# Softcap attention followed by a gated mixture of attention experts: q, k and x transposed by DMA instead of by TensorE and VectorE

## The chip, the cores and the metric

The kernel runs on one NeuronCore of a Trainium2 chip. A core has TensorE (PE, matrix products; PEld are its weight loads), VectorE (DVE), ScalarE (ACT), GpSimd (POOL) and SyncE (SP), which here only issues DMAs. Every engine works through its own instructions in order, and engines wait for each other by semaphores. DMAs are issued from an engine's instruction queue (here from SyncE and, for the weights, from GpSimd) and run on 16 DMA engines. The metric is the device time of one execution in microseconds. The time before is 442.53 us, the median of three runs (442.25 to 444.14).

## What is computed

There are 8 batches, 12 heads, 448 tokens and 64 values per head. The first part is attention with a soft cap: `scores = cap * tanh(q k^T / (8 * cap))`, with cap 30, a softmax over the keys, and a product with `v`. Its output, with the heads laid side by side, is `x`, 448 x 768 per batch. The second part works on `x`:

```python
logits = x @ w_gate                  # 4 experts, the best two kept, softmax over the two
for e in range(E):
    q, k, v = x @ wq[e], x @ wk[e], x @ wv[e]      # 64 wide
    a = softmax(causal(q @ k.T / 8))
    out += weight[e] * (a @ v @ wo[e])
```

Inputs and output are float32; the kernel computes its matrix products in float16.

## The kernel before

Work of the first part goes by pairs of heads: six pairs per batch, 48 pairs, numbered p. A main loop runs over p, one iteration per pair and a few more at the end, and the order of instructions on each engine is the order in which the program writes them (a manual schedule). Work of the second part, here called the MoE part, of batch b is cut into units (`b_v`, `b_gate`, `b_q`, `b_k`, score fills, `b_pv1`, `b_ot`, `b_wo`). A table in `batch_b` spreads these over the iterations that follow the last pair of that batch, so they run among the pairs of the next batch. Each iteration has two places for units: `w1`, between the two score fills of a pair, and `w2`, after the normalisation. After the last pair the units of the last batch run alone; this is the tail.

For one pair the steps are these.

- `load` brings q, k and v of one batch to SBUF by seven DMAs on SyncE's queue (batch 0 in four groups of seven). Four tokens of q, and three of k, lie beside each other on a partition, so that a partition reads one contiguous run. The last 64 keys of both heads come separately (`ktf`). Two sets of buffers alternate. The load of batch b + 1 is written at the start of the first iteration of batch b.
- `a_cast(p)` on GpSimd turns one pair's q, k and v to float16. It is written in iteration p - 3.
- `a_tr(p)`, written in iteration p - 2, transposes q (four products on TensorE), the tail keys (one) and k (three) into a PSUM tile `tps`. VectorE copies that to `qt` and, once per head, to a zeroed tile `kz`: the two heads share the 128 rows, so a head's keys must stand beside zeros.
- `fill0` and `fill1` compute the scores of the two heads on TensorE, four and three products with 448 columns, into the one score buffer in PSUM (four banks). `tanh` and `expo` on ScalarE turn them into unnormalised probabilities: 128 x 1792 values for the first head with both heads' tail keys, 128 x 1344 for the second.
- `a_pv` multiplies by v, with a column of ones for the sums, and `a_norm` on VectorE divides.
- `a_xt` transposes the normalised pair `xk` by four products on TensorE into `xtp`, and VectorE copies it to `xT` (line 281), with the tokens put back into their natural order: the copy writes every fourth column.

The MoE units read `xT` as soon as the last pair of a batch is there. The small PSUM tiles (`tps`, `xtp`, and all of the MoE part except its scores) take turns in two buffers. The MoE scores use the same score buffer as `fill0` and `fill1`. `b_wo` writes the output: VectorE copies to `ob`, and SyncE's queue stores it.

Of the kernel before, what the change touches and what calls it, by code (L numbers as in the profile page):

```python
# [8 lines left out]
f32 = mybir.dt.float32  # L9
f16 = mybir.dt.float16  # L10
# [6 lines left out]
def kernel(  # L17
# [13 lines left out]
    nc = tc.nc  # L31

    B, H, S, Dh = q.shape
# [62 lines left out]
    ident = const.tile([128, 128], f16, name="ident")  # L96
# [12 lines left out]
    for i in range(2):  # L109
        nc.gpsimd.memset(ktz[i], 0.0)  # L110
    for i in range(3):
        nc.vector.memset(kz[i], 0.0)
# [13 lines left out]
    cast = {}  # L126

    def a_cast(p):
        if p >= NP:
            return  # L130
        b, j = divmod(p, HP)
        qf, kf, vf, ktf, vtf = staged[b]
        h0 = 2 * j
        q16 = hd.tile([QP, QC, 2, Dh], f16, name=f"q16_{p}", tag="q16")
        k16 = hd.tile([128, KC, 2, Dh], f16, name=f"k16_{p}", tag="k16")
# [17 lines left out]
        cast[p] = (q16, k16)  # L153

    qkt = {}

    def a_tr(p):
        if p >= NP:
            return
        b, j = divmod(p, HP)  # L160
        q16, k16 = cast.pop(p)
        tps = ps_aux.tile([128, 1024], f16, name=f"tps_{p}", tag="aux")
        for c in range(QC):
            nc.tensor.transpose(  # L164
                tps[:, c * QP : (c + 1) * QP],
                q16[:, c, :, :].rearrange("p h d -> p (h d)"),
                ident[0:QP, 0:QP],
            )
        nc.tensor.transpose(tps[:, S : S + 128], ktz[b % 2][:, j, :], ident)
        for c in range(KC):  # L170
            nc.tensor.transpose(  # L171
                tps[:, S + 128 * (c + 1) : S + 128 * (c + 2)],
                k16[:, c, :, :].rearrange("p h d -> p (h d)"),
                ident,
            )
        qt = hd.tile([128, S + 128], f16, name=f"qt_{p}", tag="qt")
        nc.vector.tensor_copy(qt, tps[:, 0 : S + 128])  # L177
# [3 lines left out]
        qkt[p] = (qt, kk)  # L181

    score = {}

    def fill0(p):
        if p >= NP:
            return
        qt, kk = qkt[p]
        sc = ps_score.tile([128, 4, 512], f32, name=f"s0_{p}", tag="score")
        for c in range(KC):  # L190
            nc.tensor.matmul(  # L191
                sc[:, c, 0:S], kk[:, 0, 128 * c : 128 * (c + 1)], qt[:, 0:S],
                start=True, stop=True,
            )
        nc.tensor.matmul(sc[:, 3, 0:S], qt[:, S : S + 128], qt[:, 0:S], start=True, stop=True)  # L195
        score[(p, 0)] = sc

    def fill1(p):
        qt, kk = qkt.pop(p)
        sc = ps_score.tile([128, 4, 512], f32, name=f"s1_{p}", tag="score")  # L200
        for c in range(KC):
            nc.tensor.matmul(  # L202
                sc[:, c, 0:S], kk[:, 1, 128 * c : 128 * (c + 1)], qt[:, 0:S],
                start=True, stop=True,
            )
        score[(p, 1)] = sc

    y = {}
    pr = {}
# [53 lines left out]
        xt[p] = xk  # L263

    xT = {}

    def transpose4(ps, src):

        for n in range(4):
            nc.tensor.transpose(  # L270
                ps[:, 128 * n : 128 * (n + 1)], src(n), ident if n < 3 else swap
            )

    def a_xt(p):
        b, j = divmod(p, HP)
        if j == 0:
            xT[b] = xp.tile([128, NDC, S], f16, name=f"xT_{b}", tag="xT")
        xk = xt.pop(p)
        ps = ps_aux.tile([128, 512], f16, name=f"xtp_{p}", tag="aux")
        transpose4(ps, lambda n: xk[:, n, :, :].rearrange("p g d -> p (g d)"))  # L280
        nc.vector.tensor_copy(  # L281
            xT[b][:, j, :].rearrange("m (p c) -> m c p", c=QC),
            ps[:, 0:S].rearrange("m (c p) -> m c p", c=QC),
        )


# [160 lines left out]


    a_cast(0)
    a_cast(1)  # L450

# [30 lines left out]
    def batch_b(b):  # L482

        f = lambda fn, *a: (lambda: fn(*a))
        tab = {
            0: ([f(b_v, b, 0)], [f(b_v, b, 1), f(b_v, b, 2)]),
            1: ([f(b_v, b, 3)], [f(b_gate, b), f(b_q, b, 0)]),
            2: ([f(b_k, b, 0)], [("S", b, 0)]),
            3: ([f(b_q, b, 1)], [f(b_k, b, 1)]),
            4: ([f(b_pv1, b, 0), f(b_pv1, b, 1)], [("S", b, 1)]),  # L490
            5: (
                [f(b_pv1, b, 2), f(b_pv1, b, 3)],
                [f(b_ot, b, 0), f(b_ot, b, 1), f(b_wo, b, 0)],
            ),
            6: ([f(b_wo, b, 1)], []),
            7: ([f(b_wo, b, 2)], [f(b_wo, b, 3)]),
        }
        return tab

    sched = {}  # L500
    for b in range(B):
        for s_, (w1, w2) in batch_b(b).items():
            e_ = sched.setdefault(HP * (b + 1) + 1 + s_, ([], []))
            e_[0].extend(w1)
            e_[1].extend(w2)

    def run(units):
        for u in units:
            u()

    a_tr(0)
    a_cast(2)
    weights(0)
    a_tr(1)
    fill0(0)
    last = max(sched)
    for p in range(last + 1):
        w1, w2 = sched.get(p, ([], []))
        sB = [u for u in w2 if isinstance(u, tuple)]
        w2 = [u for u in w2 if not isinstance(u, tuple)]  # L520
        b, j = divmod(p, HP)
        if j == 0 and b + 1 < B:
            load(b + 1, [(0, HP)])
        if p < NP:
            tanh(p, 0)
            fill1(p)
        if 1 <= p <= NP:
            expo(p - 1, 1)
            a_pv(p - 1, 0)
        a_tr(p + 2)  # L530
        a_cast(p + 3)
        if 1 <= p < 4:
            weights(p)
        run(w1)
        if p < NP:
            tanh(p, 1)
        if not sB:
            fill0(p + 1)
            if p < NP:
                expo(p, 0)  # L540
        else:
            for _, bb, r in sB:
                b_fill(bb, r)
            if p < NP:
                expo(p, 0, 0, 2)
            for _, bb, r in sB:
                b_exp(bb, r)
            fill0(p + 1)
# [43 lines left out]
```

## Time and profile before

| | before |
|---|---|
| median of three runs | 442.53 us |
| the profiled execution | 441.75 us, its span 440.0 us |
| granted TensorE clock, mean | 0.939 |
| first big tanh (pair 0) starts at | 11.66 us |
| the tail, from about | 395 us |
| DMA queue of SyncE | 52,944 packets, 44.05 MB, 34.3% of 16 engines |
| VectorE, copies of `qt`, `kz` (two) and `xT` | 22.3, 16.2, 17.3 and 55.9 us |
| GpSimd idle before its q casts | 205.1 us |

The span runs from the first instruction to the last. A row of the profile's groups gives a line and an engine, what is written from what, shape and count, then the busy time, the mean of one in nanoseconds, and the idle time of that engine before these instructions with what ended it. Idle time of an engine that isn't the bottleneck costs nothing.

### The profile page before, as it was taken

How to read it: one execution, taken by the hardware profiler on the slowest of the kernel's cores; microseconds unless marked ns; L12 is line 12 of the kernel's file. 1: busy time of each engine (PE TensorE's matmuls, PEld its weight loads, DVE VectorE, ACT ScalarE, POOL GpSimd, SP SyncE). 2: the span in 40 equal slices, each digit the busy share in tenths (PEclk: the TensorE clock that was granted, in tenths of full speed). 3: DMA queues.
4: the chain of work that ended last, by engine and by line, in shares of the span. 5: the costliest groups of instructions: out<-in, count | busy, mean ns of one | idle time of the engine just before them, and what ended most of it. 6: DMA issues, size and time to landing. Idle time of an engine off the chain costs nothing.

```text
span 440.0 us, 8813 instructions
## 1 busy us (share of the span) xinstructions
PE 311.9 (71%) x3568; PEld 205.7 (47%) x3568; DVE 276.6 (63%) x693; ACT 305.7 (69%) x231; POOL 132.8 (30%) x374
## 2 busy tenths in 40 slices
PE   2676686857759677667868587686776678686865
PEld 1354464545535454444536454355544455354442
DVE  6145476567836588468755678365884687557745
ACT  1779797987757777788758877578767887584030
POOL 6793973233223323223322332233232220000000
PEclk9999899899977999999997999779999999979896
DMA  5999998001191012900184012910110001000303
GB/s 139 282 238 229 247 266 253 2 2 72 59 324 51 1 73 80 336 17 37 74 251 144 1 73 65 332 35 2 72 55 3 1 36 72 19 1 9 118 1 125
DMA packets 63497, 46.19 MB, mean 105 GB/s; under 512 B 24288, under 2 KB 59872, under 8 KB 63456
## 3 DMA queue, kind: packets, MB, share of 16 engines
q1 hardware_dynamic: 52944, 44.05, 34.3%
q0 software_dynamic: 10512, 1.58, 4.8%
q8 instruction: 28, 0.46, 0.5%
q14 instruction: 13, 0.11, 0.1%
HBM read 36.19 MB, written 11.01 MB: 107 GB/s over the span
## 4 chain that ended last, share of the span: by engine, by line
PE 45%; DVE 29%; ACT 10%; SPq 6%; issue 5%; DMA 3%; POOL 1%; DVEq 0%; ACTq 0%; POOLq 0%
PE pv L245 8%; PE s L191 6%; ACT pB L389 6%; DVE ob L443 5%; PE kps L357 4%; PE s L202 4%; DVE xT L281 4%; DVE xk L257 4%; PE vps L300 3%; PE sB L378 3%; PE qps L347 3%; PE xtp L270 2%; PE wops L438 2%; DVE kzB L361 2%; DVE kz L180 2%
## 5 line engine op out<-in xcount | busy, mean ns | idle before, releaser
L215 ACT ACTIVATE y<-s 128x1792 f16<-128x1792 f32 x96 | 141.8, 1477 | 53.6 <-PE s L195 33.5
L226 ACT ACTIVATE p<-y 128x1792 f16<-128x1792 f16 (+2 forms) x110 | 147.2, 1339 | 0.0
L136 POOL CAST q<-qf 112x512 f16<-112x512 f32 x48 | 29.5, 614 | 205.1 <-PE tps L164 176.8
L245 PEld LDWEIGHTS <-p 128*128 128x128 f16 x1536 | 66.6, 103 | 21.8 <-issue 6.2
L245 PE MATMUL pv<-v,p 128*128 128x65 f16 x1152 | 66.2, 201 | 0.8 <-ACT p L226 0.8
L281 DVE COPY xT<-xtp 128x448 f16<-128x448 f16 x48 | 55.9, 1164 | 11.4 <-PE xtp L270 11.1
L389 ACT ACTIVATE pB<-sB 128x1984 f16<-128x1984 f32 x16 | 29.2, 1824 | 46.2 <-PE sB L383 46.2
L191 PE MATMUL s<-qt,kz 128*128 128x448 f16 x144 | 40.7, 397 | 27.1 <-ACT pB L389 24.9
L245 PE MATMUL pv<-vtz,p 128*128 128x65 f16 x384 | 58.8, 199 | 0.0
L255 DVE RECIPROCAL rc<-pv 128x8 f32<-128x8 f32 x48 | 10.0, 208 | 75.6 <-PE pv L245 75.6
L438 PE MATMUL wops<-wo,oT 128*128 128x384 f16 x128 | 32.2, 348 | 18.2 <-DVE kz L180 10.3
L177 DVE COPY qt<-tps 128x576 f16<-128x576 f16 x48 | 22.3, 465 | 33.8 <-PE tps L171 33.7
L202 PE MATMUL s<-qt,kz 128*128 128x448 f16 x144 | 39.7, 389 | 4.9 <-ACT y L215 4.8
L443 DVE COPY ob<-wops 128x384 f32<-128x384 f32 (+1 forms) x64 | 34.6, 557 | 5.6 <-PE wops L438 4.6
L257 DVE TENSOR_TENSOR xk<-pv,rc 128x512 f16<-128x512 f32 x48 | 33.2, 692 | 1.7
L270 PE MATMUL xtp<-ident,xk 128*128 128x128 f16 x144 | 17.2, 232 | 23.4 <-DVE xk L257 20.6
L191 PEld LDWEIGHTS <-kz 128*128 128x128 f16 x144 | 14.7, 106 | 38.8 <-issue 32.9
L164 PE MATMUL tps<-ident,q 112*128 112x112 f16 x192 | 19.1, 227 | 13.2 <-POOL q L136 9.3
L270 PEld LDWEIGHTS <-xk 128*128 128x128 f16 x192 | 12.6, 102 | 33.9 <-DVE xk L257 25.9
L347 PE MATMUL qps<-xT,wq 128*128 128x448 f16 x96 | 23.3, 384 | 5.9 <-DVE ob L443 5.8
L300 PE MATMUL vps<-wvg,xT 128*128 128x260 f16 x192 | 26.5, 283 | 1.0
L146 POOL CAST v<-vf 128x384 f16<-128x384 f32 x48 | 24.4, 507 | 8.9 <-DMA vf<-in_v_dram 6.2
(86 smaller groups left out, 510.9 us busy)
## 6 DMA issues: line engine op xcount, KB each, us to landing
qf<-in_q_dram SPq DMA_DIRECT2D x7, 1344.0 KB, 8.5
out_dram<-ob SPq DMA_DIRECT2D x24, 384.0 KB, 2.3
kf<-in_k_dram SPq DMA_DIRECT2D x7, 1152.0 KB, 10.8
vf<-in_v_dram SPq DMA_DIRECT2D x7, 1152.0 KB, 8.3
out_dram<-ob SPq DMA_DIRECT2D x8, 192.0 KB, 2.7
ktf<-in_k_dram SPq DMA_DIRECT2D x14, 96.0 KB, 9.4
vtf<-in_v_dram SPq DMA_DIRECT2D x14, 96.0 KB, 6.8
qf<-in_q_dram SPq DMA_DIRECT2D x2, 448.0 KB, 5.1
```

The costliest lines, as they stand in the source:

```text
L191: nc.tensor.matmul(sc[:, c, 0:S], kk[:, 0, 128 * c : 128 * (c + 1)], qt[:, 0:S], start=True, stop=True,)
L202: nc.tensor.matmul(sc[:, c, 0:S], kk[:, 1, 128 * c : 128 * (c + 1)], qt[:, 0:S], start=True, stop=True,)
L215: nc.scalar.activation(yt, sc[:, 0:n, 0:S], AF.Tanh, scale=isc / capf)
L226: nc.scalar.activation(pt[:, c0:c1, :], yt[:, c0:c1, :], AF.Exp, scale=capf)
L245: nc.tensor.matmul(pv[:, g, 65 * n : 65 * n + 65], lhsT, rhs, start=(c == 0), stop=(c == KC),)
L257: nc.vector.tensor_tensor(xk.rearrange("p n g d -> p g n d"), pv[:, :, :, 0:64], rc.broadcast_to((128, 2, 4, Dh)), ALU.mult,)
L270: nc.tensor.transpose(ps[:, 128 * n : 128 * (n + 1)], src(n), ident if n < 3 else swap)
L281: nc.vector.tensor_copy(xT[b][:, j, :].rearrange("m (p c) -> m c p", c=QC), ps[:, 0:S].rearrange("m (c p) -> m c p", c=QC),)
L300: nc.tensor.matmul(ps, xT[b][:, j, WIN[n] : WIN[n] + 128], wvg[:, j, :], start=(j == 0), stop=(j == NDC - 1))
L389: nc.scalar.activation(pb[:, 64:2048], s.pop(("sc", r))[:, 0:1984], AF.Exp, scale=isc)
L438: nc.tensor.matmul(ps, s["oT"][r][:, w : w + 128], wo2[r][:, f * (D // 2) : (f + 1) * (D // 2)], start=(r == 0), stop=(r == 1),)
L443: nc.vector.tensor_copy(ob[lo:128, f * (D // 2) : (f + 1) * (D // 2)], ps[lo:128, :])
```

## The change

`a_tr` no longer uses TensorE, PSUM and VectorE. It issues two transposing DMAs on SyncE's queue: one for q (112 partitions x 512 columns), one for k (128 x 896). So that the transposed keys stand beside zeros, the zeros are put in before: a constant tile `kin` (three buffers, set to zero once by VectorE) has seven blocks of 128 columns, three per head and one for the tail keys of both, and `a_cast` on GpSimd writes the keys of a head into its half of the columns. The cast of k is thereby two instructions instead of one. `fill` reads `kt` (7 blocks) and `qt` where these DMAs land.

`a_xt` issues two transposing DMAs, one for the first three windows of tokens (128 x 384) and one for the last 64 tokens, to a new tile `xp`. A new step `a_xu`, on GpSimd and one iteration later, copies `xp` to `xT` and restores the order of the tokens. The MoE table is written anew: its units come half an iteration later, the last ones closer together, and within an iteration `a_xt` now stands before the units of `w2`. Ahead of the loop `a_tr(1)` moves before `a_cast(2)`.

```diff
-    ktz = [const.tile([128, HP, 128], f16, name=f"ktz{i}") for i in range(2)]
+    kin = [const.tile([128, 7, 128], f16, name=f"kin{i}") for i in range(3)]
-    kz = [const.tile([128, 2, KM], f16, name=f"kz{i}") for i in range(3)]
...
     def a_cast(p):
-        nc.gpsimd.tensor_copy(
-            k16, kf[:, h0 : h0 + 2, :].rearrange("p h (c d) -> p c h d", c=KC)
-        )
-        kt = ktz[b % 2]
-        nc.gpsimd.tensor_copy(kt[0:64, j, 0:Dh], ktf[0:64, j, :])
-        nc.gpsimd.tensor_copy(kt[64:128, j, Dh:128], ktf[64:128, j, :])
+        kk = kin[p % 3]
+        for g in range(2):
+            nc.gpsimd.tensor_copy(
+                kk[:, KC * g : KC * (g + 1), Dh * g : Dh * (g + 1)],
+                kf[:, h0 + g, :].rearrange("p (c d) -> p c d", c=KC),
+            )
+            nc.gpsimd.tensor_copy(
+                kk[64 * g : 64 * (g + 1), 2 * KC, Dh * g : Dh * (g + 1)],
+                ktf[64 * g : 64 * (g + 1), j, :],
+            )
...
     def a_tr(p):
-        tps = ps_aux.tile([128, 1024], f16, name=f"tps_{p}", tag="aux")
...
-        qt = hd.tile([128, S + 128], f16, name=f"qt_{p}", tag="qt")
-        nc.vector.tensor_copy(qt, tps[:, 0 : S + 128])
-        kk = kz[p % 3]
-        nc.vector.tensor_copy(kk[0:64, 0, :], tps[0:64, S + 128 : S + 512])
-        nc.vector.tensor_copy(kk[64:128, 1, :], tps[64:128, S + 128 : S + 512])
+        q16 = cast.pop(p)
+        qt = hd.tile([128, S], f16, name=f"qt_{p}", tag="qt")
+        nc.sync.dma_start_transpose(
+            qt.rearrange("m (c p) -> m c p", c=QC), q16.rearrange("p c h d -> p (c h d)")
+        )
+        kt = hd.tile([128, 7, 128], f16, name=f"kt_{p}", tag="kt")
+        nc.sync.dma_start_transpose(kt, kin[p % 3].rearrange("p c m -> p (c m)"))
...
     def a_xt(p):
-        ps = ps_aux.tile([128, 512], f16, name=f"xtp_{p}", tag="aux")
-        transpose4(ps, lambda n: xk[:, n, :, :].rearrange("p g d -> p (g d)"))
-        nc.vector.tensor_copy(
+        xp_ = hd.tile([128, S], f16, name=f"xp_{p}", tag="xp")
+        nc.sync.dma_start_transpose(
+            xp_[:, 0:KM].rearrange("m (n t) -> m n t", n=3),
+            xk[:, 0:3, :, :].rearrange("p n g d -> p (n g d)"),
+        )
+        nc.sync.dma_start_transpose(
+            xp_[:, KM:S].unsqueeze(1), xk[64:128, 3, :, :].rearrange("p g d -> p (g d)")
+        )
+        xun[p] = xp_
+
+    def a_xu(p):
+        b, j = divmod(p, HP)
+        nc.gpsimd.tensor_copy(
             xT[b][:, j, :].rearrange("m (p c) -> m c p", c=QC),
-            ps[:, 0:S].rearrange("m (c p) -> m c p", c=QC),
+            xun.pop(p).rearrange("m (c p) -> m c p", c=QC),
         )
...
         a_tr(p + 2)
         a_cast(p + 3)
+        if 2 <= p <= NP + 1:
+            a_xu(p - 2)
...
             a_pv(p - 1, 1)
             a_norm(p - 1)
-        run(w2)
         if 1 <= p <= NP:
             a_xt(p - 1)
+        run(w2)
```

More of the change, by code (lines that the diff above doesn't have):

```diff
@@ L108 @@
     pB = [const.tile([128, 64 + 1984], f16, name=f"pB{i}") for i in range(2)]
-    for i in range(2):
-        nc.gpsimd.memset(ktz[i], 0.0)
     for i in range(3):
-        nc.vector.memset(kz[i], 0.0)
+        nc.vector.memset(kin[i], 0.0)
     for i in range(2):
@@ L134, in a_cast @@
         q16 = hd.tile([QP, QC, 2, Dh], f16, name=f"q16_{p}", tag="q16")
-        k16 = hd.tile([128, KC, 2, Dh], f16, name=f"k16_{p}", tag="k16")
         nc.gpsimd.tensor_copy(
@@ L152, in a_cast @@
         nc.gpsimd.tensor_copy(vt_[64:128, j, 1, 0:Dh], vtf[64:128, j, :])
-        cast[p] = (q16, k16)
+        cast[p] = q16
     qkt = {}
@@ L159, in a_tr @@
             return
-        b, j = divmod(p, HP)
-        q16, k16 = cast.pop(p)
-        tps = ps_aux.tile([128, 1024], f16, name=f"tps_{p}", tag="aux")
[L163 to L175, printed above, removed]
@@ L176, in a_tr @@
-        qt = hd.tile([128, S + 128], f16, name=f"qt_{p}", tag="qt")
-        nc.vector.tensor_copy(qt, tps[:, 0 : S + 128])
-        kk = kz[p % 3]
-        nc.vector.tensor_copy(kk[0:64, 0, :], tps[0:64, S + 128 : S + 512])
-        nc.vector.tensor_copy(kk[64:128, 1, :], tps[64:128, S + 128 : S + 512])
-        qkt[p] = (qt, kk)
+        q16 = cast.pop(p)
[3 more added lines that the diff above has]
+        )
@@ L183, with fill @@
+        kt = hd.tile([128, 7, 128], f16, name=f"kt_{p}", tag="kt")
+        nc.sync.dma_start_transpose(kt, kin[p % 3].rearrange("p c m -> p (c m)"))
+        qkt[p] = (qt, kt)
     score = {}
-    def fill0(p):
+    def fill(p, g):
         if p >= NP:
             return
-        qt, kk = qkt[p]
-        sc = ps_score.tile([128, 4, 512], f32, name=f"s0_{p}", tag="score")
+        qt, kt = qkt[p]
+        sc = ps_score.tile([128, 4, 512], f32, name=f"s{g}_{p}", tag="score")
         for c in range(KC):
[L191 to L206, printed above, removed]
+            nc.tensor.matmul(sc[:, c, 0:S], kt[:, KC * g + c, :], qt, start=True, stop=True)
+        if g == 0:
+            nc.tensor.matmul(sc[:, KC, 0:S], kt[:, 2 * KC, :], qt, start=True, stop=True)
@@ L208 @@
+        score[(p, g)] = sc
     y = {}
@@ L265 @@
     xT = {}
+    xun = {}
     def transpose4(ps, src):
@@ L484, in batch_b @@
         f = lambda fn, *a: (lambda: fn(*a))
[L485 to L497, printed above, removed]
+        tab = [
+            [],
+            [f(b_v, b, 0), f(b_v, b, 1)],
+            [f(b_v, b, 2), f(b_v, b, 3)],
+            [f(b_gate, b), f(b_q, b, 0)],
+            [f(b_k, b, 0)],
+            [("S", b, 0)],
+            [f(b_q, b, 1)],
+            [f(b_k, b, 1)],
+            [f(b_pv1, b, 0), f(b_pv1, b, 1)],
+            [("S", b, 1)],
+            [f(b_pv1, b, 2), f(b_pv1, b, 3)],
+            [f(b_ot, b, 0), f(b_ot, b, 1), f(b_wo, b, 0), f(b_wo, b, 1)],
+            [f(b_wo, b, 2), f(b_wo, b, 3)],
+        ]
         return tab
@@ L501 @@
     for b in range(B):
[L502 to L505, printed above, removed]
+        for i, units in enumerate(batch_b(b)):
+            sched.setdefault(2 * (HP * (b + 1) + 1) + i, []).extend(units)
     def run(units):
@@ L511 @@
     a_tr(0)
+    a_tr(1)
     a_cast(2)
     weights(0)
-    a_tr(1)
-    fill0(0)
-    last = max(sched)
+    fill(0, 0)
+    last = max(sched) // 2
     for p in range(last + 1):
-        w1, w2 = sched.get(p, ([], []))
+        w1, w2 = sched.get(2 * p, []), sched.get(2 * p + 1, [])
         sB = [u for u in w2 if isinstance(u, tuple)]
@@ L525 @@
             tanh(p, 0)
-            fill1(p)
+            fill(p, 1)
         if 1 <= p <= NP:
@@ L537 @@
         if not sB:
-            fill0(p + 1)
+            fill(p + 1, 0)
             if p < NP:
@@ L547 @@
                 b_exp(bb, r)
-            fill0(p + 1)
+            fill(p + 1, 0)
             if p < NP:
```

## The prediction

> **What bounds the kernel now.** First the page's table of busy time by engine.
>
> ```profile
> PE 311.9 (71%) x3568; PEld 205.7 (47%) x3568; DVE 276.6 (63%) x693; ACT 305.7 (69%) x231; POOL 132.8 (30%) x374
> ```
>
> Three engines stand near 70% and none is full, so I read ScalarE's own timeline, away from the MoE work and inside it. Columns: start, length, engine, line, what, and idle time before it.
>
> ```profile
> 33.22 1.31 ACT L226 ACTIVATE p<-y 128x1344 f16<-128x1344 f16 x1
> 34.43 1.28 ACT L215 ACTIVATE y<-s 128x1344 f16<-128x1344 f32 x1
> 35.60 1.70 ACT L226 ACTIVATE p<-y 128x1792 f16<-128x1792 f16 x1
> 37.19 1.66 ACT L215 ACTIVATE y<-s 128x1792 f16<-128x1792 f32 x1
> 38.73 1.33 ACT L226 ACTIVATE p<-y 128x1344 f16<-128x1344 f16 x1
> ```
>
> Here one head pair takes 38.73 - 33.22 = 5.5 us and ScalarE never waits: PE and VectorE, transposes included, are wholly behind it. The big tanh of pairs 36 to 42, with MoE work between, starts at 301.40, 307.23, 315.57, 322.92, 335.46, 340.99 and 350.44: 49.0 us for six pairs. ScalarE's own work there is 6 x 5.5 plus two MoE exponentials at 1.8, 36.7 us. The other 12.3 us are waits, the same as in the list of waits (us in total, times, longest):
>
> ```profile
> ACT pB L389 <- PE sB L383: 46.2, 16, 5.7
> ACT y L215 <- PE s L195: 33.5, 34, 9.6
> ACT eexp L322 <- DVE lg L311: 21.1, 7, 12.3
> SPq L446 <- DVE ob L443: 280.5, 25, 33.9
> ```
>
> So only iterations with MoE work can be shortened, up to 12 us per batch. The last line matters as much: today the SyncE queue does nothing but load and store, waits 280 us for stores, and so runs its loads far ahead. The SyncE timeline:
>
> ```profile
> 17.62 0.59 SPq L74 DMA_DIRECT2D qf<-in_q_dram  x1
> ...
> 34.62 0.89 SPq L90 DMA_DIRECT2D vtf<-in_v_dram  x1
> ...
> 119.27 0.54 SPq L74 DMA_DIRECT2D qf<-in_q_dram  x1
> 119.90 0.71 SPq L77 DMA_DIRECT2D kf<-in_k_dram  x1
> 120.70 3.79 SPq L82 DMA_DIRECT2D ktf<-in_k_dram  x1
> 124.55 1.94 SPq L83 DMA_DIRECT2D ktf<-in_k_dram  x1
> 126.60 1.30 SPq L84 DMA_DIRECT2D vf<-in_v_dram  x1
> 128.41 2.31 SPq L89 DMA_DIRECT2D vtf<-in_v_dram  x1
> 130.78 0.61 SPq L90 DMA_DIRECT2D vtf<-in_v_dram  x1
> ```
>
> One batch's load holds SyncE 12.1 us (four such: 10.9 to 12.3, so 11.5), about 340 GB/s for its 4.1 MB. The load at 119.27 belongs to iteration 18, whose tanh starts at 147.80: it ran 28 us ahead, and cost nobody anything.
>
> **What the change removes.** VectorE loses, per pair, 0.465 (qt) + 0.338 + 0.361 (kz) + 1.164 (xT) = 2.33 us, 112 us of its 277. PE loses twelve transposes; by the pieces of the chain (tps 0.20 + 0.06 + 0.18, xtp 0.38) 0.82 us per pair. Rows:
>
> ```profile
> L281 DVE COPY xT<-xtp 128x448 f16<-128x448 f16 x48 | 55.9, 1164 | 11.4 <-PE xtp L270 11.1
> L177 DVE COPY qt<-tps 128x576 f16<-128x576 f16 x48 | 22.3, 465 | 33.8 <-PE tps L171 33.7
> ```
>
> What that is worth lies between 0 and 12.3 us per batch. What stays behind ScalarE is the chain in the iterations with an MoE score fill: kps 1.15, kzB 0.62 + 0.23 (+ 0.55), sB 1.4, of which the half exponential covers 0.95. I leave 2 us of waits for each of the two and a little for the rest: 4.3 us remain, 8 go, and a batch would take 41 us if the transposes cost nothing.
>
> **What it adds on GpSimd.** The k cast in two (from the 64- and 384-column casts, 0.23 and 0.51 us, 0.35 each at 192: +0.2) and the reordering copy, 448 columns: 0.6 us by the cast rows, 1.5 if the strided writes hurt as on VectorE (1.16 against 0.46 for more columns). 2.6 us per pair become 3.4 to 4.3, below 5.5; GpSimd idles 205 us before its q casts. Taken as hidden. Its new wait (x landed) has the next pair's casts behind it; they are needed over an iteration later. If that cover went, it would be 1 us per pair, 48 in all.
>
> **What it adds on SyncE.** Four transposing DMAs per pair, and no row shows one. A 128-column block of two-byte values is 256 B per row: q has 112 x 4 = 448 such pieces, k 128 x 7 = 896, x 128 x 3 + 64 = 448; 1,792 in all, 0.46 MB. Low end: by bytes at the load's 340 GB/s, 1.35 us per pair moving, with issue at 0.6 us each (startup rows: 0.39 to 0.66), 2.4 us of SyncE. High end: the 256 B pieces of the ktf load at its worst, 4.32 us for 384, 11.25 ns each, 20 us per pair; that row is mostly back-pressure of the loads ahead. Between them lies the nearest row of small packets:
>
> ```profile
> q0 software_dynamic: 10512, 1.58, 4.8%
> ```
>
> 4.8% of 16 x 440 us is 338 us, 32 ns per packet of 150 B, 2.0 ns over 16 engines: 3.6 us per pair. I take it, and that SyncE is held while a transpose's pieces are pushed: q 1.5, k 2.4, x 1.4 + 0.7, 6.0 us per pair; landing 2 us later (2.3 for a store).
>
> Against this stand two statements of the Trainium skill that disagree. Its page Advanced Engine Details and Errata, section X-Bar Transpose (TRN2), holds transposing DMAs as fast as others, 350 to 400 GB/s: an estimate of 1.3 us per pair, and a result near 436. Its page VectorE: DVE Perf Modes, section The three transpose paths, gives 1309 ns for one 128x128 block by DMA against 390 on TensorE, and tells authors to use TensorE where PSUM will do: 14 blocks per pair would be 18 us, an estimated 1,000 us in all. No row here shows either.
>
> **Where it meets the path.** SyncE works in order. The x transposes wait for VectorE's normalisation late in the iteration, and behind them stand the next load, the next pair's q and k, and the stores. So loads lose their lead. Three places:
>
> 1. Startup. Batch 0's load holds SyncE to 18.2; now q and k of pairs 0 and 1 follow (7.8, to 26), then the load of batch 1 (17.9 us today beside the weight loads; later these are thinner, 15: to 41), then pair 2 (3.9, landing 2, fill 0.9): the big tanh of pair 2 at 48 instead of
>
> ```profile
> 24.85 1.66 ACT L215 ACTIVATE y<-s 128x1792 f16<-128x1792 f32 x1 [1.23 <-PE s L195]
> ```
>
> +23 us. Bounds: 37 (+12) and, with k at the high price, +60.
>
> 2. The six later load iterations. The load starts about 1 us after the iteration does, then q, k of the pair after next: 1 + 11.5 + 3.9 + 2 = 18.4; its fill is wanted at 5.6 + 3.5 = 9. PE stands 9.4 us, with the MoE units queued behind it. Late next is x of the pair before: behind those transposes it lands at 16.4 + 2.1 + 2 = 20.5, when the first MoE unit that reads it is due at 18.4 + 0.8 + 0.5 + 0.8; nothing more is added. Batch: 41 + 9.4 = 50.4. SyncE's own sum gives the same: 6 x 6.0 + 11.5 + four stores at 0.6 = 49.9. Before, pairs 6 to 42 took (350.44 - 50.80) / 6 = 49.9. Change: about 0.5 x 6 = +3, or 0 as the first of the six has little MoE work.
>
> 3. The last batch, pairs 42 to 47, has no load: 41 against 47, -6. Then the tail, 45 us: transposing x of the last pair costs 2.1 + 2 + 0.6 against 0.4 + 1.16, +3; the shift of MoE work by half an iteration adds nothing, as the units follow each other there.
>
> Sum: 440.0 + 23 + 0 - 6 + 3 = 460 us of span; with the 1.75 us around it (441.75) 462. The runs' median, 442.53, is 0.8 above the profiled run: **463 us**.
>
> **Rivals.**
>
> *The transposes are dearer, and SyncE or the DMA rate becomes the bound.* For: 256 B pieces, four short transfers each with its own end, on the queue that loads use; against: 6.0 us per pair already counts issue and moving one after the other. At 9 us per pair a batch is 54 + 14 = 68: 6 x 18 + 9 (last batch) + 30 (startup) + 3 = +150, 592 us. At 20 us it would be above 1,000.
>
> *The other side: SyncE isn't held.* If issuing returns after 0.6 us and the pieces move beside the next issue, q and k hold it 1.2 us. Startup +12; at a load 1 + 11.5 + 1.2 + 2 = 15.7 against 9, batch 47.7, 6 x -2.2 = -13; -6; +2. Sum -5: 435 span, 437. It decides at about 1.7 us for q and k together; if all 12.3 us of waits went too, another 4 per batch, 410. For: startup issues took 0.6 us without regard to size; against: the loads in mid-kernel held SyncE as long as their data took.
>
> *The two cancel* between these, within 0.5% (2 us, about what a measurement of this kernel can tell from none): 440 to 445.
>
> **How the numbers follow.** Forecast (4 to 8 us per pair, 445 to 520): 0.42. Dearer (above 520): 0.35. Not held: 0.16. Cancelled: 0.07. So faster 0.16, same 0.07, slower 0.77. The range: 433 leaves out about half of the cheap case (0.08), 640 the third of the dear case beyond 10 us per pair (0.12).
>
> **What would show it.** Right: transposing DMAs on SyncE of 1 to 2.5 us each; tanh of pair 2 near 48 us; PE's score fill waiting for a DMA once per batch for some 9 us; VectorE near 165 us busy; iterations without load or MoE fill at 5.5 to 6.5 us. Wrong towards slow: PE waiting for qt or kt in every iteration, SyncE never waiting for VectorE's xk. Wrong towards fast: transposes of 0.6 us issue. Also wrong: GpSimd's copy above 3 us, so that vps waits for xT.

## The result and the profile after

| | before | after |
|---|---|---|
| median | 443.33 us (442.25 to 446.05) | 501.04 us (498.60 to 505.11) |
| ratio | | 1.13 (95%: 1.121 to 1.139) |
| the profiled execution, its span | 441.75, 440.0 us | 505.11, 503.3 us |
| granted TensorE clock, mean | 0.939 | 0.801 |

The kernel became 13% slower. The forecast was 463 us: the sign was right, the size was not. Ratios here leave out executions that the chip disturbed; medians are over all executions.

The page of after: busy time by engine, SyncE's DMA queue (packets, MB, share of 16 engines), and the chain that ended last, by engine.

```profile
PE 311.5 (62%) x2992; PEld 195.1 (39%) x2992; DVE 171.8 (34%) x501; ACT 305.7 (61%) x231; POOL 186.1 (37%) x468
...
q1 hardware_dynamic: 145104, 66.09, 55.5%
...
SPq 31%; PE 29%; ACT 19%; DMA 9%; DVE 7%; issue 3%; POOL 1%; DVEq 0%; POOLq 0%; ACTq 0%
```

VectorE lost 105 us of work and no engine gained as much, yet the span grew by 63. The largest share of the chain now belongs to SyncE's queue (SPq), which computes nothing.

**Where the 63 us lie.** ScalarE's big tanh (128 x 1792) starts once per pair, so its starts in the two timelines divide the span:

| stretch | before, us | after, us | change | forecast |
|---|---|---|---|---|
| start to pair 2 | 24.85 | 47.39 | +22.5 | +23 |
| pair 2 to 6 | 25.95 | 25.04 | -0.9 | 0 |
| pair 6 to 42, six batches | 299.64 | 345.94 | +46.3 | 0 to +3 |
| pair 42 to 47 | 41.41 | 36.44 | -5.0 | -6 |
| the tail | 48.15 | 48.49 | +0.3 | +3 |

One row failed, the third: 57.7 us per batch, against 49.9 before and 50.4 forecast. The next table divides it: the mean time from the big tanh of a pair to the next one, by the pair's place in its batch, over the six batches. e1 and e2 are experiments told below (no loads; more output buffers).

| pair in batch | 0 | 1 | 2 | 3 | 4 | 5 | sum |
|---|---|---|---|---|---|---|---|
| before | 5.80 | 7.87 | 7.06 | 12.63 | 6.97 | 9.61 | 49.9 |
| after | 5.99 | 17.78 | 8.85 | 9.75 | 6.70 | 8.59 | 57.7 |
| e1, no later loads | 5.86 | 7.30 | 5.75 | 9.57 | 6.01 | 8.57 | 43.1 |
| e2, six output buffers | 5.73 | 17.87 | 6.61 | 9.38 | 6.30 | 8.34 | 54.2 |

Column 1 is the load's stall, column 2 something that follows it. In the waits of after (us in total, times, longest):

```profile
POOL xT L268 <- DMA xp<-xk: 254.7, 46, 15.9
...
ACT y L191 <- PE s L181: 113.4, 35, 26.5
...
PE s L179 <- DMA kt<-kin: 94.0, 9, 26.8
DVE ob L430 <- DMA out_dram<-ob: 66.9, 7, 13.9
```

The third line is the forecast stall: PE's score fill waits for the transposed keys. Of its nine waits two fall into the startup (26.8 and 7.3 us) and six stand behind the six loads of this stretch, 7.7 to 13.5 us each, 9.7 in the mean. The fourth was not forecast: VectorE waits for an output buffer that a store still holds. SyncE's own waits:

```profile
SPq L257 <- DVE xk L233: 68.2, 25, 5.4
SPq L433 <- DVE ob L430: 27.0, 9, 21.6
```

Before, SyncE waited 280.5 us for `ob`, so it ran ahead of everybody. Now it waits for the normalised pair, and everything else in its queue waits with it. SyncE's timeline of after (start, length, engine and line, what) around the first load of that stretch:

```profile
74.27 1.19 SPq L257 DMA_TRANSPOSE xp<-xk  x1
75.51 2.06 SPq L261 DMA_TRANSPOSE xp<-xk  x1
77.63 0.58 SPq L74 DMA_DIRECT2D qf<-in_q_dram  x1
...
88.89 0.63 SPq L90 DMA_DIRECT2D vtf<-in_v_dram  x1
89.63 1.43 SPq L164 DMA_TRANSPOSE qt<-q  x1
91.17 1.42 SPq L168 DMA_TRANSPOSE kt<-kin  x1
```

ScalarE's timeline beside it, which ends each line with the idle time before it:

```profile
78.24 1.66 ACT L191 ACTIVATE y<-s 128x1792 f16<-128x1792 f32 x1
...
96.41 1.66 ACT L191 ACTIVATE y<-s 128x1792 f16<-128x1792 f32 x1 [12.54 <-PE s L181]
```

The load is written first in iteration 6, whose tanh starts at 72.43. SyncE comes to it at 77.63, directly behind the x transposes of the iteration before, and the transposes of q and k of pair 8 come directly behind the load, at 89.63. Pair 8's tanh follows at 96.41, 18.2 us after pair 7's. The other five loads begin 4.0 to 4.4 us behind the tanh of their iteration.

Then the stall has a tail. The chain that ended last in after, in order of time, near another load:

```profile
361.93 1.18 SPq L257
...
363.16 1.22 SPq L261
...
364.43 0.57 SPq L74
...
376.77 1.56 SPq L164
...
378.43 1.54 SPq L168
...
380.07 1.21 SPq L257
...
381.33 1.22 SPq L261
...
382.64 2.55 DMA out_dram<-ob
385.22 0.05 DVEq L430
385.31 0.57 DVE ob L430
385.93 2.76 PE vps L287 x12
```

For 21 us the chain never leaves SyncE: x transposes, load, transposes of q and k, transposes of x, and only then a store of an earlier batch. VectorE's copy to `ob` needs the buffer of that store, and PE's first MoE product (`vps`) needs the PSUM buffer which that copy empties.

### The profile page after: what moved, and what is told of

It reads as the page before. It is cut to its first block, busy times and chain, and to the rows that moved or that the text cites. A ratio compares the mean times of both kernels' runs of the same rounds, so it can differ in the third digit from the quotient of the medians.

```text
span 503.3 us, 7991 instructions
## 1 busy us (share of the span) xinstructions
PE 311.5 (62%) x2992; PEld 195.1 (39%) x2992; DVE 171.8 (34%) x501; ACT 305.7 (61%) x231; POOL 186.1 (37%) x468
## 4 chain that ended last, share of the span: by engine, by line
SPq 31%; PE 29%; ACT 19%; DMA 9%; DVE 7%; issue 3%; POOL 1%; DVEq 0%; POOLq 0%; ACTq 0%
ACT y L191 9%; PE s L179 8%; SPq L82 7%; ACT pB L376 5%; PE vps L287 5%; SPq L89 5%; PE pv L221 4%; ACT p L202 4%; DMA kt<-kin 3%; SPq L257 3%; DMA out_dram<-ob 3%; SPq L261 3%; SPq L83 3%; SPq L168 3%; SPq L164 3%
## 5 line engine op out<-in xcount | busy, mean ns | idle before, releaser
L179 PE MATMUL s<-qt,kt 128*128 128x448 f16 x288 | 96.2, 457 | 150.2 <-DMA kt<-kin 94.0
L268 POOL COPY xT<-xp 128x448 f16<-128x448 f16 x48 | 56.9, 1185 | 254.8 <-DMA xp<-xk 254.7
L179 PEld LDWEIGHTS <-kt 128*128 128x128 f16 x288 | 31.2, 112 | 183.5 <-DMA kt<-kin 96.4
L221 PEld LDWEIGHTS <-p 128*128 128x128 f16 x1536 | 79.1, 114 | 30.8 <-issue 19.6
L221 PE MATMUL pv<-v,p 128*128 128x65 f16 x1152 | 77.6, 217 | 2.0 <-DVE xk L233 1.1
L221 PE MATMUL pv<-vtz,p 128*128 128x65 f16 x384 | 68.3, 215 | 0.0
L430 DVE COPY ob<-wops 128x384 f32<-128x384 f32 (+1 forms) x64 | 33.0, 554 | 77.2 <-DMA out_dram<-ob 66.9
L139 POOL CAST kin<-kf 128x192 f16<-128x192 f32 x96 | 33.2, 345 | 2.1 <-DMA kt<-kin 1.8
L287 PEld LDWEIGHTS <-xT 128*128 128x128 f16 x192 | 22.8, 122 | 16.2 <-POOL q L134 4.2
L143 POOL CAST kin<-ktf 64x64 f16<-64x64 f32 x96 | 22.6, 235 | 3.0
L181 PE MATMUL s<-qt,kt 128*128 128x448 f16 x48 | 22.6, 470 | 0.0
L425 PEld LDWEIGHTS <-oT 128*128 128x128 f16 x128 | 11.6, 99 | 26.2 <-issue 13.8
```

The costliest lines, as they stand in the source:

```text
L139: nc.gpsimd.tensor_copy(kk[:, KC * g : KC * (g + 1), Dh * g : Dh * (g + 1)], kf[:, h0 + g, :].rearrange("p (c d) -> p c d", c=KC),)
L179: nc.tensor.matmul(sc[:, c, 0:S], kt[:, KC * g + c, :], qt, start=True, stop=True)
L221: nc.tensor.matmul(pv[:, g, 65 * n : 65 * n + 65], lhsT, rhs, start=(c == 0), stop=(c == KC),)
L268: nc.gpsimd.tensor_copy(xT[b][:, j, :].rearrange("m (p c) -> m c p", c=QC), xun.pop(p).rearrange("m (c p) -> m c p", c=QC),)
L287: nc.tensor.matmul(ps, xT[b][:, j, WIN[n] : WIN[n] + 128], wvg[:, j, :], start=(j == 0), stop=(j == NDC - 1))
L425: nc.tensor.matmul(ps, s["oT"][r][:, w : w + 128], wo2[r][:, f * (D // 2) : (f + 1) * (D // 2)], start=(r == 0), stop=(r == 1),)
```

## The experiments

Diffs are against the kernel after, unless said otherwise. The explanations on trial: **queue**, SyncE's order makes the load iterations stall; **clock**, the transposes kept TensorE busy and without them its granted clock falls; **lead**, sharper than queue, that it is x's wait for the normalisation which takes SyncE's lead away.

**e1. No loads after the first batch.**

```diff
+        if b > 0:
+            staged[b] = staged[0]
+            return
```

> The changed kernel without the loads of batches 1 to 7: every batch is computed from the q, k and v of batch 0, so 28.9 MB of reads are left out. All else stays. Theory 'queue' (what costs time is that loads and transposing DMAs share SyncE's queue in order): the big tanh of pair 2 starts at about 34 us (47.4 minus the 13.4 us of the load) instead of 47.4, the waits of about 10.6 us in each of six batches go, and the 4.2 us of the iteration after: 501 - 13 - 6 x 13 = about 410 us. Theory 'clock' (what costs time is TensorE at half clock, because its transposes are gone): the waits of the score fills for kt go, but iterations without MoE work stay at a granted clock of about 0.67, and a batch stays near 49 us: 440 to 450. Theory 'transposes are dear in themselves' (the DMA engines can't move the pieces in time): PE goes on waiting for kt, above 460.

Measured: 408.11 us (ratio 0.925, 0.915 to 0.936; two executions). Every batch is computed from batch 0's q, k and v, so this kernel leaves out part of the task. All transposes are still there, and the kernel is 93 us faster than after. The waits of e1 show the key wait only twice, 26.5 us before the first fill and 3.5 us once more, and in no later batch:

```profile
PE s L182 <- DMA kt<-kin: 30.0, 2, 26.5
```

So the transposing DMAs alone cost little in the batches, and what costs there is their meeting with the loads. A batch takes 43.1 us. This is not what the kernel would take with free loads, as less data moves.

**e2. Six output buffers instead of three.**

```diff
-    outp = ctx.enter_context(tc.tile_pool(name="outp", bufs=3))
+    outp = ctx.enter_context(tc.tile_pool(name="outp", bufs=6))
```

> The changed kernel with six output buffers (ob) instead of three. Theory 'queue', second half: in the iteration after each load VectorE waits for a store (66.9 us in 7 waits) that stands on SyncE behind load and transposes, and the MoE products wait for VectorE; with a free buffer this goes and the iteration after the stall falls from 9.8 to about 6 us: 501 - 6 x 4 = about 477. Rival: that iteration is long because TensorE runs at half clock after its stall and the x of the pair before is late anyway: VectorE's wait goes, but the time stays within 5 us of 501.

Measured: 481.67 us (1.094, 1.084 to 1.104), 19 us less than after. VectorE's wait for `ob` is gone from the list; column 2 of the table falls from 8.85 to 6.61 and column 1 stays at 17.9. The wait for stores is a real second cost, and smaller than the stall.

**e3. Eight transposes on TensorE per pair again, read by nobody.**

```diff
+        for c in range(QC):
+            nc.tensor.transpose(tps[:, c * QP : (c + 1) * QP], q16[:, c, :, :]..., ident[0:QP, 0:QP])
+        for c in range(4):
+            nc.tensor.transpose(tps[:, S + 128 * c : S + 128 * (c + 1)], kin[p % 3][:, c, :], ident)
```

> The changed kernel with eight transposes per pair put back on TensorE (four of q16, four blocks of kin) into a PSUM tile that nobody reads; VectorE copies nothing. Theory 'clock': the granted clock of the stretch from pair 2 to pair 6, without MoE work and without loads, goes from 0.67 back to about 0.95, the whole from 0.80 to 0.9, and the time falls by 2 to 4 us per batch in spite of 0.5 us more work per pair: 480 to 490. Theory 'queue': the clock falls because PE stands still while it waits for DMAs, and transposes that are done before don't fill that gap: clock and time stay, 498 to 510.

Measured: 503.72 us (1.143, 1.132 to 1.154), no better than after. The busy time of after in the stretch of pairs 2 to 6. Columns: stretch, length, busy time of PE, PEld, VectorE, ScalarE and GpSimd (instructions), then the granted clock, the DMA share and GB/s.

```profile
47.40:78.20 30.80, 22.05 (x204) 13.77 (x202) 4.50 (x10) 28.50 (x20) 20.54 (x46) 0.67 0.78 90
```

The same stretch of e3, with the same columns:

```profile
47.40:78.20 30.80, 20.66 (x244) 14.47 (x243) 4.50 (x10) 28.30 (x21) 22.16 (x50) 0.78 0.85 99
```

The clock rises from 0.67 to 0.78 (over the whole run from 0.801 to 0.841), PE does more work in less busy time, and ScalarE does the same work in the same stretch. The clock came back only in part (the expectation named 0.95), and the added transposes are work for PE too. So a higher clock bought nothing that the time shows, and the clock falls as the main cause; that it costs nothing is not shown.

**e4. The loads after the first on GpSimd's queue.**

```diff
+        eng = nc.sync if b == 0 else nc.gpsimd
...
-            nc.sync.dma_start(
+            eng.dma_start(
```

> The changed kernel with the loads of batches 1 to 7 issued from GpSimd's queue instead of SyncE's; all of its work is done. Theory 'queue': transposes no longer stand behind a load; if GpSimd issues a load in about 6 us, the waits for kt mostly go: 420 to 440. Rival 'engines': loads and transposes share the 16 DMA engines whichever queue they come from, so kt still lands late during a load and the waits stay above 5 us each: 470 to 500; or GpSimd, held by the issue, is late with its casts, and the fills wait for those.

Measured: 458.23 us (1.039, 1.023 to 1.055; two executions): between the two expectations, 43 us under after and 50 over e1. A batch takes 49.8 us, and PE's waits for keys behind the six loads are 5.9 us in the mean, against 9.7 in after. The waits of e4:

```profile
PE s L180 <- DMA kt<-kin: 73.4, 9, 26.1
...
DVE ob L431 <- DMA out_dram<-ob: 27.8, 6, 7.3
```

The SyncE timeline of e4 while a load, issued from 73.89 on, moves its data:

```profile
73.72 1.18 SPq L258 DMA_TRANSPOSE xp<-xk  x1
74.94 2.36 SPq L262 DMA_TRANSPOSE xp<-xk  x1
77.41 1.36 SPq L165 DMA_TRANSPOSE qt<-q  x1
79.31 3.92 SPq L169 DMA_TRANSPOSE kt<-kin  x1
83.33 1.78 SPq L258 DMA_TRANSPOSE xp<-xk  x1
85.16 3.82 SPq L262 DMA_TRANSPOSE xp<-xk  x1
```

Nothing stands ahead of the transposes now, and yet they hold SyncE for up to 3.9 us instead of 1.2. So the order in the queue is one part of the stall, and sharing the DMA engines with the load is likely another. How the 50 us over e1 divide was not measured: GpSimd itself is held 5.6 us (73.89 to 79.53) by issuing the load, ahead of the next casts. The Trainium skill, DMA: Bandwidth & Descriptors, section Rules for kernel authors, says that spreading DMAs over several issuing engines brings no bandwidth and only saves the sequencer's issue time; here the 43 us show how much it can be worth to take a load out of a queue in which other work stands behind it, and the 3.9 us agree with data that still shares its way.

**e5. From the kernel before: x alone by DMA**, with GpSimd's reordering copy and the new MoE table; q and k stay on TensorE.

```diff
     def a_xt(p):
-        transpose4(ps, lambda n: xk[:, n, :, :].rearrange("p g d -> p (g d)"))
-        nc.vector.tensor_copy(
+        nc.sync.dma_start_transpose(...)
+        nc.sync.dma_start_transpose(...)
...
+    def a_xu(p):
+        nc.gpsimd.tensor_copy(
...
         a_cast(p + 3)
+        if 2 <= p <= NP + 1:
+            a_xu(p - 2)
```

> The kernel before with only x transposed by DMA and put in order on GpSimd, and the new MoE table; q and k stay on TensorE and VectorE. Theory 'queue': the loads lose their lead (each stands behind the transposes of the pair before), but no score fill waits for SyncE, so startup is as before (big tanh of pair 2 near 25 us) and the kt waits are absent; what remains is VectorE's wait for the store behind the load, 4 us or less in six batches, against some 3 us per batch that the xT copies and PE's waits for xk give back: 430 to 450. If x alone by DMA cost as much as its half of the transposes, 470.

Measured: 486.22 us (1.096, 1.088 to 1.104). The time lies 36 us above the range that was expected and 16 above the 470 of the other case: x alone, a quarter of the transposed pieces, brings most of the loss. By ScalarE's timeline the place is another: the tanh of pair 2 starts at 24.16, as before, and the first stall comes behind the load of batch 1. GpSimd's timeline of e5 there (the last bracket is the idle time before):

```profile
46.24 1.17 POOL L292 COPY xT<-xp 128x448 f16<-128x448 f16 x1 [14.69 <-DMA xp<-xk]
...
50.21 0.65 POOL L136 CAST q<-qf 112x512 f16<-112x512 f32 x1
```

ScalarE's timeline of e5, three pairs after pair 2:

```profile
53.97 1.66 ACT L215 ACTIVATE y<-s 128x1792 f16<-128x1792 f32 x1 [13.11 <-PE s L195]
```

x's transposes stand behind the load on SyncE and are issued at 38.55. GpSimd's copy waits 14.7 us for them, the casts of the next pair stand behind that copy on GpSimd, and TensorE, VectorE and ScalarE wait for the casts. Pairs 2 to 6 take 36.47 us instead of 25.95, about 10 of the 44 us by which e5's span is longer.

The six batches hold 40 us more, and there the chain is another. The waits of e5:

```profile
POOL xT L292 <- DMA xp<-xk: 259.1, 42, 14.7
...
DVE ob L454 <- DMA out_dram<-ob: 34.9, 6, 8.4
...
PE vps L311 <- DVE ob L454: 29.1, 6, 7.2
...
PE tps L164 <- POOL q L136: 20.7, 4, 12.8
```

GpSimd's wait for x recurs (first line), but PE waits for casts only four times (last line). Behind later loads PE waits before the first MoE product, `vps`, for VectorE's `ob` and so for the store, as in after. x itself comes hardly earlier: at the load of iteration 18 GpSimd's copy of the last x ends at about 199 us and the product starts at 199.51, so a freed `ob` alone would have brought little there.

**e6. q and k alone by DMA**; x is transposed by TensorE and VectorE as before.

```diff
     def a_xt(p):
-        nc.sync.dma_start_transpose(...)
-        nc.sync.dma_start_transpose(...)
+        transpose4(ps, lambda n: xk[:, n, :, :].rearrange("p g d -> p (g d)"))
+        nc.vector.tensor_copy(
...
     def a_xu(p):
+        pass
```

> The changed kernel with x transposed by TensorE and copied to xT by VectorE as before, so that only q and k go by DMA; the new MoE table stays, and the transposes of x stand after the units of w2 as before. Theory 'queue': the startup (+22) and the wait of about 10 us per load stay, since they come from q and k behind the load, only shorter by the 2.4 us of SyncE that x took; SyncE is free between, so loads may run ahead of the program by up to an iteration and the wait may shrink to 3 to 6 us: 460 to 485. If x by DMA is what delays (it ties SyncE to VectorE's normalisation in every iteration), the waits at the loads go almost wholly: 430 to 450.

Measured: 436.11 us (0.972, 0.965 to 0.979), faster than before, although its startup loses what after's loses (pair 2 at 47.18). A batch takes 45.6 us. PE waits for keys only in the startup (26.4 and 7.4 us) and behind no later load, as the waits of e6 show:

```profile
PE s L179 <- DMA kt<-kin: 33.8, 2, 26.4
```

In SyncE's own waits the largest beside that for `ob` is now one for free `qt` buffers, which PE's fills return:

```profile
SPq L164 <- PE s L179: 80.2, 17, 9.4
```

SyncE's timeline of e6, the first DMA of the load of iteration 18:

```profile
155.85 0.58 SPq L74 DMA_DIRECT2D qf<-in_q_dram  x1
```

ScalarE's timeline of e6, the big tanh of that iteration:

```profile
166.40 1.66 ACT L191 ACTIVATE y<-s 128x1792 f16<-128x1792 f32 x1 [0.17 <-PE s L181]
```

The load starts 10.5 us ahead of the tanh (the six loads 7.1 to 10.5). In after the same load started 4.0 us behind its tanh (186.88 against 182.91). With x out of the queue SyncE waits only for free `qt` buffers and runs ahead again. Three quarters of the pieces against e5's one, and 50 us less time.

**e7. Each load in thirds, over three iterations, the transposes of pairs 0 and 1 between the groups of the first load, six output buffers.**

```diff
-    load(0, [(0, 1), (1, 1), (2, 2), (4, 2)])
+    load(0, [(0, 1), (1, 1)])
...
+    a_tr(0)
+    load(0, [(2, 2)])
+    a_tr(1)
+    load(0, [(4, 2)])
...
-        if j == 0 and b + 1 < B:
-            load(b + 1, [(0, HP)])
+        if j < 3 and b + 1 < B:
+            load(b + 1, [(2 * j, 2)])
```

> The changed kernel, all by DMA as there, with three rearrangements on SyncE: the load of the next batch is issued in thirds (two pairs each) in the first three iterations instead of whole in the first; the transposes of pairs 0 and 1 stand between the groups of batch 0's load; six output buffers. Theory 'queue': no transpose then stands behind more than 4.2 us of loads, which 1.5 iterations of lead cover; the first big tanh starts at about 16 us instead of 28.5, and batches take 42 to 45 us: 405 to 420, below the kernel before. Rival 'engines': the same bytes share the same 16 engines and SyncE's work per batch is the same 44 us, so the waits only spread over three iterations: 450 to 480.

Measured: 470.43 us (1.057, 1.051 to 1.063), 11 us better than e2. The first tanh came 13 us earlier (14.99), but pair 6's only 2 us earlier than e2's (69.96 against 71.87), and a batch took 53.2 us against 54.2. The key wait in the list of waits of e7, which in after was 94.0 us in 9 pieces:

```profile
PE s L181 <- DMA kt<-kin: 85.4, 21, 13.3
```

From pair 6 on, the waits add up to 49 us in 16 pieces, against 59 us in six pieces in e2. Cutting the block spreads the wait over more iterations and takes a small part of it away, and the startup's gain is 7.8 us at pair 2 (39.22, e2 47.04) and 1.9 at pair 6. The block's length is not the main cause.

**e8. From the kernel before: the new MoE table alone.** The table as in the change, nothing else.

> The kernel before with nothing changed but the MoE table (units half an iteration later, the last ones closer together). Every theory that ascribes the loss to the DMAs expects 440 to 446, the same as before. If the new table were part of the loss or of the gain, it would show here: above 450, or below 435.

Measured: 442.01 us (0.995, 0.991 to 0.999). The table explains none of the loss.

**e9. x's transposes and the reordering copy one iteration later.** The table gets two more empty half iterations, as its units need x.

```diff
         tab = [
             [],
+            [],
+            [],
...
         a_tr(p + 2)
-        a_cast(p + 3)
         if 2 <= p <= NP + 1:
-            a_xu(p - 2)
+            a_xt(p - 2)
+        a_cast(p + 3)
+        if 3 <= p <= NP + 2:
+            a_xu(p - 3)
...
-        if 1 <= p <= NP:
-            a_xt(p - 1)
```

> The changed kernel with the transposes of x issued later on SyncE: after those of q and k of the next iteration instead of before them, when the normalisation is long done; the copy on GpSimd and the MoE units come one iteration later too. Bytes, number of DMAs and SyncE's work are the same. Theory 'lead' (the wait for VectorE's normalisation at the end of each iteration keeps SyncE from running more than 1.5 iterations ahead of the score fills, less than a load takes): SyncE gains about one iteration of lead, the waits of 10.6 us at the six loads shrink to 2 to 4, startup stays, the wait for the stores stays in part: 450 to 465. Rival 'volume' (SyncE's 44 us per batch, or the bytes, are the limit): the order among them doesn't matter, 490 to 510.

Measured: 450.34 us (1.017, 1.009 to 1.024), 51 us less than after with the same DMAs, the same bytes and the same copies. In SyncE's own waits of e9 the one for the normalised pair, 68.2 us in after:

```profile
SPq L257 <- DVE xk L233: 12.2, 9, 4.3
```

Its SyncE timeline at the same load as above:

```profile
67.83 1.21 SPq L261 DMA_TRANSPOSE xp<-xk  x1
69.09 0.58 SPq L74 DMA_DIRECT2D qf<-in_q_dram  x1
...
82.07 1.33 SPq L164 DMA_TRANSPOSE qt<-q  x1
```

The load starts 1.2 us ahead of its iteration's tanh (70.33), against 5.2 us behind it in after: 6.4 us earlier. The other five start from 1.9 us ahead to level with it, against 4.0 to 4.4 us behind. Column 1 of the table becomes 11.07 us, 6.7 us less than after. A batch takes 48.6 us. And the stores are on time again: VectorE's wait for `ob`, 66.9 us in after, in the waits of e9:

```profile
DVE ob L430 <- DMA out_dram<-ob: 0.9, 2, 0.7
```

PE's waits for keys behind the six loads are 2.8 to 7.6 us, 5.1 in the mean: the time came at the lower edge of what was expected, and the waits stayed longer than the 2 to 4 us that were named.

This edit loosens two ties at once, SyncE's to VectorE and GpSimd's to x; in the load iterations q's transpose follows the last piece of the load within 0.2 us (81.95 to 82.07 here, 89.52 to 89.63 in after), so there it is SyncE's order that decides. A run with GpSimd's copy alone moved later would separate the two; there is none.

**e10. e6 with loads in thirds (iterations 1 to 3, behind the casts), the early transposes of e7 and six output buffers.**

```diff
-        if j == 0 and b + 1 < B:
-            load(b + 1, [(0, HP)])
...
         a_cast(p + 3)
+        if 1 <= j < 4 and b + 1 < B:
+            load(b + 1, [(2 * j - 2, 2)])
```

> Only q and k by DMA (x as before, new MoE table), and SyncE's queue rearranged: the transposes of pairs 0 and 1 between the groups of batch 0's load, later loads in thirds in the second to fourth iteration of a batch, after the transposes; six output buffers. Theory 'lead': the first big tanh starts at about 16 us instead of 28, pair 2 near 30 instead of 47, and batches stay at 45 us or a little less: 436 - 15 = 415 to 422, below the kernel before. Rival: pieces of a load among the transposes cost as much as whole loads did in the changed kernel: 430 to 445.

Measured: 415.41 us (0.935, 0.929 to 0.942): faster than both kernels, and the best of the study that does the whole computation. In the profiled execution, the longest of the four (423.45 us), pair 2 starts at 33.70 instead of 47.18, pair 6 at 65.10 instead of 73.83, and a batch takes 45.7 us as in e6. So the gain lies in the startup. A similar rearrangement gave e7 2 us at pair 6, and 9 here, where x is not in the queue.

**e11. e9 with six output buffers.**

> The changed kernel with both: x one iteration later on SyncE, and six output buffers. If the two causes are separate ('lead' and the store that VectorE waits for), their gains add up: e9's time minus about 15 to 20 us, 430 to 445. If the store's wait was only a consequence of the late queue, six buffers add less than 5 us to e9.

Measured: 447.14 us (1.008, 1.003 to 1.012), 3 us less than e9, which their spreads hardly separate, where the same edit brought 19 on after. Of the two cases of the expectation the second came: the gains do not add up. With e9's wait for `ob` at 0.9 us there was nothing left to gain. The late stores are a consequence of the late queue.

## Why the prediction was right or wrong

- **Startup, right, the closeness in part luck.** Pair 2 at 47.39, forecast 48. The terms were off both ways: q and k of two pairs took 6.9 us of SyncE (17.73 to 24.68; forecast 7.8), and the load 13.3 (24.73 to 38.00; forecast 15), but from there to the tanh it took 9.4 us (forecast 6.8), as q and k behind the load held SyncE 2.4 and 3.0 us. The 18.2 us at which the prediction lets batch 0's load end is the end of the next load's first DMA; batch 0's own ended at 17.6.
- **SyncE 6.0 us per pair, a little too dear.** In quiet stretches a transpose holds SyncE 1.2 us, whatever its size (`qt` 1.20, `kt` 1.25, `xp` 1.18 and 1.22): 4.85 us. The small-packet row was a fair substitute, but the price goes by instruction and not by piece. SyncE's own sum per batch becomes 6 x 4.85 + 11.5 + 2.4 = 43 us; added up over the timeline from pair 6 to 42, where transposes beside a load take longer, it is 45.8. A batch took 57.7, so SyncE was not full: it waited.
- **The dearer rival, wrong; "not held", wrong too.** q and k hold SyncE 2.45 us, on the slow side of the 1.7 us from which that rival would decide. Its 437 us took 0.6 us per issue.
- **"PE stands 9.4 us", right in mechanism and, partly by luck, in size.** PE's six waits have a mean of 9.7 us; by the table the stall is 17.78 - 7.30 = 10.5. But the load starts 4.0 to 5.2 us behind its iteration's tanh, not 1: the normalisation ends about 1.5 us behind it (361.91 against 360.46), and x's two transposes, 2.5 us, stand between that and the load and were left out. On the other side the fill was wanted later than assumed: in e1 the tanh of the pair after next comes 13.2 us behind the iteration's (columns 0 and 1), where the prediction's 9 and 0.9 us for the fill give 9.9.
- **"Nothing more is added", the step that failed.** It followed x to its first reader and stopped there. Behind x in the queue stood the stores, behind a store VectorE's `ob`, behind that PE's PSUM buffer: column 2, 8.85 - 5.75 = 3.1 us per batch, where the prediction has nothing: the largest of the misses between the 50.4 us that were forecast and the 57.7 measured. e2's spare buffers give back 2.2 of these, 3.4 us per batch with the other pairs, and 19 us of the run. The waits of before had no such line, as a store was issued as soon as its data was there; that a late SyncE would make one had to be worked out from the three `ob` buffers.
- **"41 us if the transposes cost nothing", too low.** e1 has 43.1, and it moves less data. Together: 2.1 (base) + 1.1 (stall) + 3.1 (the next pair) + 1.0 (the other four) = 7.3 us per batch, 44 of the 46.3 us.
- **The lead taken as given.** The prediction worked out that the load starts 1 us into its iteration and did not ask what fixed that. e9 asks: the same work, x one iteration later, and 51 us are gone. e6 says it from the other side: without x in the queue the kernel beats before.
- **GpSimd, right in busy time, wrong on its queue.** The copy is 1.18 us (forecast 0.6 to 1.5), and hidden as work. "They are needed over an iteration later" did not cover a copy that waits 15 us with the casts behind it; e5 shows the whole chain at its first load. What this wait costs in after, beside SyncE's, no run separated.
- **Last batch and tail.** -5.0 against -6, and +0.3 against +3 (the -6 covers six gaps from pair to pair, the row five). VectorE at 171.8 us busy against 165.

e5 and e6 do not add up to after: on their spans +44.0 and -8.6 give +35, and the change gave +63. A likely reason, which no run isolates: together q's and k's transposes stand in a queue that x holds back, which neither half has.

## What to carry to other kernels

Here a queue that only loaded and stored ran ahead at no cost, and its lead was worth more than its busy time showed. Before putting a DMA into it that depends on computed data, ask how late that data is in the loop, what stands behind it in the queue, and who waits for that, step by step until an engine is reached that has slack; then issue it where its input is long done, even an iteration later. When the parts of a change depend on the loop differently, as q and k (ready early) and x (ready late), try them apart.

## What was unexpected in the hardware

The landing times of the DMAs of after (count, median us from issue to landing):

```profile
xp<-xk SPq DMA_TRANSPOSE x96, 2.4
...
kt<-kin SPq DMA_TRANSPOSE x48, 2.9
qf<-in_q_dram SPq DMA_DIRECT2D x2, 224.0 KB, 2.9
```

- A transposing DMA was cheap here and nearly flat: seven blocks of keys land in 2.9 us, the x transposes of one to three blocks in 2.4. The keys are 224 KB (128 x 896 values of two bytes), and plain loads of that size (q of one pair, from DRAM) landed in 2.9 us as well. The two statements of the Trainium skill that disagreed can be weighed now. VectorE: DVE Perf Modes, section The three transpose paths, has 1309 ns for one block, which is near the issue time of a whole transpose here (1.2 us) and far too dear for each of seven. Advanced Engine Details and Errata, section X-Bar Transpose (TRN2), calls transposes as fast as other DMAs: nearer, by the 2.9 us of both, but without the 1.2 us per instruction, where plain DMAs at the start held SyncE 0.4 to 0.66 us.
- Beside a load the same instruction holds SyncE for up to 3.9 us (e4).
- The reordering copy costs GpSimd 1185 ns from SBUF and cost VectorE 1164 ns from PSUM: the strided write, not the engine, seems to set it, which was not tried.
- Transposes that nobody reads went with a rise of the granted clock from 0.67 to 0.78 in the stretch of pairs 2 to 6 (e3). The Trainium skill, TensorE: Matmul & The Clock Gate, Part 4, says that transposes do not count as busy in the same way; here they counted for something. A batch in e1 still took 2 us more than the forecast base; whether the clock is why stays open.
